# Layer 1's first product also of seven block products, summed in PSUM, with float32 weights kept in DRAM and GpSimd out of the weights

## The chip, the cores and the metric

The kernel runs on one core of a Trainium2 chip. The metric is the device time of one execution in microseconds (us), the median of three runs. The engines are named by their short names where rows are quoted: PE is TensorE's matmul, PEld its weight load, DVE VectorE, ACT ScalarE, POOL GpSimd, SP the engine that issues nearly all DMAs.

## The reference

Attention for 2 batches of 8 heads with 768 tokens of 64 values, masked by a hash bucket, and behind it two feed-forward layers on 1536 tokens of 512 values with 2048 hidden ones. The weights of both layers are float64.

```python
x = attn_out.transpose(0, 2, 1, 3).reshape(1536, 512)
h = x @ w_in;  sp = log1p(exp(min(h, 20)));  x = (h * tanh(sp)) @ w_out     # layer 1
h = x @ w_in2; return (h - tanh(h)) @ w_out2                                # layer 2
```

## The kernel before

Every float32 operand is kept as a high part, rounded to the matmul's float32r format, and a low part (the rest); a product is three matmuls: high by high, high by low, low by high. ScalarE makes high parts (a CAST), VectorE or GpSimd low parts (a subtraction).

**The order** is made by a planner (`Plan`). Each operation is handed in with an engine, an assumed cost, a key (a due time) and the buffers it reads and writes; the planner runs a list schedule over them, and the program is emitted in the order that comes out. Engines then work strictly in that order. The constants (UNIT, STEP, JIT, ...) set keys and costs only. SP's DMAs stand in one queue in that order too.

**Weights** arrive as 512 KB of float64 for 128 hidden units (`raw`). A conversion to float32 is four steps: VectorE masks the high word (TENSOR_SCALAR), VectorE merges sign and exponent (SCALAR_TENSOR_TENSOR), ScalarE scales the low word (ACTIVATE), and a sum joins them (on VectorE it shows as CUSTOM_DVE_ANT_0 or ISA, 128x1024 uint16). For layer 1 (`convert`) a split into high and low part follows at once, and all 32 tiles stay in SBUF (pools wa, wb, wc). For layer 2 (`fetch`) the sum is on GpSimd (L940), the float32 result is stored in DRAM, and each unit loads it back.

**Layer 1** (`feed_forward`, `hidden`, `outer`) goes over three blocks of 512 tokens and, in each, over 16 slices m of 128 hidden units: 12 matmuls of 512 columns make h (L823 to L825), ScalarE applies Mish and rounds (L838, L839), VectorE takes the low part (L842), and 12 matmuls of 512 columns add to four accumulators (L859).

**Layer 2** (`second_layer`, `unit`) goes over two halves of 768 tokens and 8 units of 256 hidden units each. A unit's first product is a 2x2 block product, made of seven block products (`product`) instead of eight: of each 6 matmuls with 384 columns (L1092 to L1094). That needs sums of the token blocks (t1 to t4, 22 GpSimd operations a half, in `tokens`) and of the weight blocks (s1 to s4, four GpSimd operations of 256 columns a unit). Five sums of products are made by VectorE from PSUM and SBUF (`plus`). Behind Tanh, 36 matmuls of 512 columns follow (L1143).

**PSUM**: tag s is one double bank, first for scores, then two accumulators; tag pt has six banks. In layer 1 two of the six are accumulators, in layer 2 four, which leaves two for the first product.

Of the kernel before, what the change touches and what calls it, by code (L numbers as in the profile page):

```python
# [39 lines left out]
N_A = 5  # L40
N_B = 3
N_PRE = 2
POOL_C = ((1, 4), (3,))
POOL_LAST = ((4,), (4,))
# [4 lines left out]

G_BUFS, E_BUFS, GX_BUFS, F_BUFS = 3, 3, 2, 2  # L50
T_BUFS, P_BUFS, U_BUFS = 3, 6, 3
# [3 lines left out]
EPS = 0.005  # L55
SPARE = 1
LATE = 0.22
LATS = 0.15
LATC = 1.0
# [6 lines left out]
MTICK = 5.53  # L66
# [13 lines left out]
OUT_LAG = 13.0  # L80
RAW = 12.0
C0 = 6.0
WB0 = 6

UNIT = 15.7
STEP = 1.06
OUT2 = 20.0
JIT = 18.0
DGL = 0.75
DY = 0.6  # L90
LATO = 1.0
FETCH = 30.0
CONV0 = -10.0
CONV2 = 5.2
TOK0 = 75.0
TOK1 = 70.0
UNIT0 = 0.0
TREL = 0.0
# [25 lines left out]
class Plan:  # L124
# [46 lines left out]
    def order(self):  # L171
        free, ready, done, queue = {}, {}, [], {}
# [23 lines left out]
        while len(done) < len(self.ops):  # L196
# [15 lines left out]
            o.start, o.end = t, t + o.cost  # L212
# [32 lines left out]
def tile_lsh_attention_moe(  # L245
# [52 lines left out]
    def slots(m0, m1):  # L298
        return " ".join(f"w{n}{m}" for m in range(m0, m1) for n in "io")

    for name, m0, m1 in (("wb", N_A, N_A + N_B), ("wc", N_A + N_B, KF)):
        for tag in slots(m0, m1).split():
            room(name, tag, 1)

    wd = (("a2", "a20 a21 a22 a23", 1), ("t2", "t2h t2l t3h t3l t4h t4l", 1), ("g2", "gh gl", 4), ("f2", "f2", 3))
    for name, tags, n in wd:
        for tag in tags.split():
            room(name, tag, n)

    room("raw", "raw", 2)  # L310
# [7 lines left out]
            ("const", "", 1), ("xy", "", 1), ("wa", slots(0, N_A), 1), ("t", "t", T_BUFS),   # L318
            ("g", "ph", G_BUFS), ("e", "pl", E_BUFS), ("f", "f", F_BUFS),
# [27 lines left out]
    def dma(nbytes, key, out, in_, reads=(), writes=(), release=0.0):  # L347

        op("DMA", max(0.55, nbytes / 180e3), key, lambda: nc.sync.dma_start(out=out(), in_=in_()), reads, writes, release=release)  # L349
# [317 lines left out]
    def finish(g, half, u, key):  # L667

        b, hp = pairs[g]
        r = rs[g, half]  # L670
        op(
            "POOL", 1.07, key + 0.2,
            lambda: nc.gpsimd.tensor_tensor(out=u(), in0=u(), in1=r(), op=ALU.mult),
            [r], [(u, 0), (u, 1)],
        )
        t0 = b * NT + half * TB
        cols = slice(t0 * P, (t0 + TB) * P)
        op("POOL", 0.5, key + 0.3, lambda: pool_copy(xh[hp][:, cols], u()), [(u, 0), (u, 1)], x_tok("xh", hp, t0, TB))
# [206 lines left out]

# [388 lines left out]
```

## Time and profile before

| | |
|---|---|
| time, median of 3 runs | 765.64 us (765.47 to 766.31) |
| the profiled execution | 765.25 us, its span 763.4 us |
| TensorE, VectorE, ScalarE, GpSimd busy | 746.7, 576.3, 462.5, 321.4 us |
| attention, layer 1, layer 2 | to about 235, 501 and 763 us |

The time is the device's for the whole execution; the span runs from the first to the last instruction. Busy time is the time in which an engine has at least one instruction under way; consecutive instructions of TensorE and VectorE overlap, so what one costs in a row of them is the distance of their starts, which is less than its duration.

### The profile page before, as it was taken

How to read it: one execution, taken by the hardware profiler on the slowest of the kernel's cores; microseconds unless marked ns; L12 is line 12 of the kernel's file. 1: busy time of each engine (PE TensorE's matmuls, PEld its weight loads, DVE VectorE, ACT ScalarE, POOL GpSimd, SP SyncE). 2: the span in 40 equal slices, each digit the busy share in tenths (PEclk: the TensorE clock that was granted, in tenths of full speed). 3: DMA queues.
4: the chain of work that ended last, by engine and by line, in shares of the span. 5: the costliest groups of instructions: out<-in, count | busy, mean ns of one | idle time of the engine just before them, and what ended most of it. 6: DMA issues, size and time to landing. Idle time of an engine off the chain costs nothing.

```text
span 763.4 us, 11533 instructions
## 1 busy us (share of the span) xinstructions
PE 746.7 (98%) x3853; PEld 650.9 (85%) x3853; DVE 576.3 (75%) x1044; ACT 462.5 (61%) x926; POOL 321.4 (42%) x346
## 2 busy tenths in 40 slices
PE   7999999999999899999999999999999999999998
PEld 5999999998988688888888888888887898889986
DVE  6999899899899898854443576669788877767743
ACT  6999899899897556653242435366455545445432
POOL 4787677677665200012222377434456321213000
PEclk9999999999999999999999999999999999999999
DMA  6674675665667630026565435632211124211002
GB/s 174 163 177 129 143 168 135 145 154 126 153 260 242 255 131 1 27 73 190 142 193 152 143 89 176 224 124 72 81 56 56 56 83 157 65 55 57 28 1 82
DMA packets 35559, 94.24 MB, mean 123 GB/s; under 512 B 5798, under 2 KB 8742, under 8 KB 35500
## 3 DMA queue, kind: packets, MB, share of 16 engines
q1 hardware_dynamic: 34924, 92.89, 41.6%
q8 instruction: 30, 0.49, 0.3%
q10 hardware_dynamic: 576, 0.62, 0.2%
q14 instruction: 29, 0.24, 0.1%
HBM read 63.01 MB, written 11.58 MB: 98 GB/s over the span
## 4 chain that ended last, share of the span: by engine, by line
PE 80%; DVE 8%; ACT 5%; DMA 3%; SPq 2%; issue 2%; ACTq 0%; DVEq 0%
PE pt L1143 11%; PE s L859 8%; PE pt L859 8%; PE pt L823 5%; PE pt L825 5%; PE pt L824 5%; PE pt L600 5%; PE s L1143 5%; PE pt L1092 4%; PE pt L1094 4%; PE pt L1093 4%; PE s L539 3%; PE s L540 3%; PE pt L578 3%; PE pt L579 3%; SPq L349 2%
## 5 line engine op out<-in xcount | busy, mean ns | idle before, releaser
L940 POOL TENSOR_TENSOR t<-t,raw 128x512 uint32<-128x512 uint32 x32 | 45.3, 1415 | 164.0 <-ACT raw L935 118.8
L543 DVE TENSOR_SCALAR_CACHE_REDUCE p<-s 128x768 f32<-128x768 f32 x93 | 88.3, 950 | 15.0 <-PE s L540 14.6
L565 ACT ACTIVATE p<-p,mn 128x768 f32<-128x768 f32 x96 | 90.5, 943 | 3.8 <-DVE p L543 2.1
L600 PE MATMUL pt<-cst,p 128*128 128x128 f32 x576 | 87.2, 274 | 2.3 <-ACT p L565 1.4
L898 POOL TENSOR_TENSOR f<-wi 128x256 f32<-128x256 f32 x32 | 30.4, 955 | 121.4 <-DVE a L898 33.2
L619 DVE TENSOR_TENSOR pl<-pt,ph 128x384 fp32r<-128x384 f32 x146 | 78.0, 548 | 4.7 <-ACT ph L616 3.7
L600 PEld LDWEIGHTS pt<-cst,p 128*128 128x128 f32 x576 | 70.6, 140 | 11.4 <-ACT f L608 3.3
L823 PE MATMUL pt<-xh,wi 128*128 128x512 f32 x192 | 75.6, 394 | 0.0
L825 PE MATMUL pt<-xh,wi 128*128 128x512 f32 x192 | 75.4, 393 | 0.0
L824 PE MATMUL pt<-xl,wi 128*128 128x512 f32 x192 | 75.3, 392 | 0.0
L616 ACT CAST ph<-pt 128x384 fp32r<-128x384 f32 x146 | 68.0, 480 | 9.2 <-PE pt L600 4.6
L578 PE MATMUL pt<-ph,vt 128*128 128x384 f32 x192 | 71.3, 371 | 0.4 <-DVE pl L619 0.4
L539 PE MATMUL s<-b,a 128*128 128x384 f32 x186 | 67.8, 364 | 1.7 <-DVE p L543 1.4
L838 ACT ACTIVATE f<-pt 128x512 f32<-128x512 f32 x34 | 20.3, 598 | 77.8 <-PE pt L825 77.6
L842 DVE TENSOR_TENSOR pl<-f,ph 128x512 fp32r<-128x512 f32 x34 | 28.4, 835 | 50.6 <-ACT ph L839 50.3
L579 PE MATMUL pt<-pl,vt 128*128 128x384 f32 x192 | 65.5, 341 | 0.0
L540 PE MATMUL s<-d,c 77*128 77x384 f32 (+1 forms) x186 | 63.2, 340 | 0.1
L859 PE MATMUL s<-ph,wo 128*128 128x512 f32 x192 | 59.7, 391 | 2.8 <-DVE wo L807 2.8
L859 PE MATMUL pt<-ph,wo 128*128 128x512 f32 x192 | 59.1, 389 | 0.0
L1107 ACT CAST gh<-pl 128x384 fp32r<-128x384 f32 x64 | 32.8, 514 | 29.6 <-DVE pl L898 28.9
L612 POOL TENSOR_TENSOR pl<-f,ph 128x384 fp32r<-128x384 f32 x46 | 48.5, 1054 | 2.5
L1105 ACT ACTIVATE f<-pl 128x384 f32<-128x384 f32 x48 | 25.2, 526 | 38.0 <-DVE pl L898 34.5
(256 smaller groups left out, 2060.5 us busy)
## 6 DMA issues: line engine op xcount, KB each, us to landing
wi<-in_moe_w_in_dram SPq DMA_DIRECT2D x16, 512.0 KB
wo<-in_moe_w_out_dram SPq DMA_DIRECT2D x16, 512.0 KB
raw<-in_moe_w_in_dram SPq DMA_DIRECT2D x16, 512.0 KB
w<-t SPq DMA_DIRECT2D x32, 256.0 KB
raw<-in_moe_w_out_dram SPq DMA_DIRECT2D x16, 512.0 KB
wi<-w SPq DMA_DIRECT2D x16, 512.0 KB
wo<-w SPq DMA_DIRECT2D x16, 512.0 KB
b<-kh SPq DMA_DIRECT2D x30, 192.0 KB
```

The lines of the kernel that those rows point to most:

```text
L539: nc.tensor.matmul(o, a()[:, tok], b_()[:, kc], start=True, stop=False)
L540: nc.tensor.matmul(o, c_()[used, tok], d_()[used, kc], start=False, stop=True)
L543: nc.vector.tensor_scalar(out=out, in0=in_, scalar1=MASKED, scalar2=None, op0=ALU.min, op1=ALU.min, accum_out=low)
L565: lambda: nc.scalar.activation(out=p(), in_=p(), func=AF.Exp, bias=mn(), scale=-1.0, accum_out=sm()[:, h, t:t + 1],),
L578: nc.tensor.matmul(o()[:, :HB], vt()[:, c, :], ph()[:, :HB], start=(c == 0), stop=False)
L579: nc.tensor.matmul(o()[:, :HB], vt()[:, c, :], pl()[:, :HB], start=False, stop=(c == NT - 1))
L600: nc.tensor.transpose(pt()[:, t * P:(t + 1) * P], pc[:, c * P:(c + 1) * P], ident)
L823: nc.tensor.matmul(h(), w()[:, 0, c], xh[kk][:, cols], start=(kk == 0), stop=False)
L824: nc.tensor.matmul(h(), w()[:, 0, c], xl[kk][:, cols], start=False, stop=False)
L825: nc.tensor.matmul(h(), w()[:, 1, c], xh[kk][:, cols], start=False, stop=(kk == KD - 1))
L859: nc.tensor.matmul(o, x, y, start=st and i == 0, stop=sp and i == 2)
L1143: nc.tensor.matmul(o, x()[:, i, c], w()[:, y], start=m == 0 and k == 0, stop=m == KF - 1 and k == 2)
```

## The change

Layer 1 takes the form that layer 2 has: two halves of 768 tokens, 8 units each, units numbered 0 to 31 over both layers. In its first half the first four units (PLAIN) make the 2x2 block product of eight block products; all others of seven. Layer 1's second product (`outer1`) works on 768 columns at once, as a matmul of 512 and one of 256 with the same weights. It has four accumulators in the 512s and two shared banks for the 256s, so two pt banks are left here too.

The seven products are summed in PSUM where that is possible: a copy by ScalarE starts a bank, and later products accumulate in it; two `plus` sums of five remain on VectorE. Layer 1's weights are converted to float32 for the first half, stored in DRAM, and loaded again for the second; each half splits them anew. All sums of conversions and of weight blocks are on VectorE, but those of units 0 and 1 (N_PRE), whose eight conversions lie in attention and end on GpSimd. The last pair's `finish` is on VectorE and ScalarE. Costs and keys in the planner are new; it also counts VectorE and GpSimd as slowing each other.

```diff
-POOL_LAST = ((4,), (4,))
+POOL_LAST = ((4,), ())
+SUMS = ("DVE", 0.34)
@@ order: VectorE and GpSimd slow each other in the plan
+            if o.eng == "DVE" and inside(o):
+                took += SLOW * min(took, max(0.0, free.get("POOL", 0.0) - t))
@@ finish
+        eng, cost, e = ("DVE", 0.55, nc.vector) if last else ("POOL", 1.07, nc.gpsimd)
@@ to_float, the conversion's last step (before: GpSimd in layer 2)
+        eng, cost, e = ("POOL", 1.45, nc.gpsimd) if pooled else ("DVE", 0.62, nc.vector)
+        op(eng, cost, key + 0.6, lambda: e.tensor_tensor(out=t(), in0=t(), in1=word(0), op=ALU.add), [raw], [tok], lat=LATF)
@@ unit_weights: layer 1's first half converts and stores, all others load
+            if (layer, sb) == (1, 0):
+                for side in range(2):
+                    i = 2 * part + side
+                    when = at(CONV_A + (4 * n + i) * CONV_S) if n < N_PRE else unit_at(n) - CONV1 + i * CSTEP
+                    to_float(
...
+                dma(P * DM * 8, when + CSTEP, lambda d=d: d.rearrange("p (m f) -> p m f", m=2), w32[part], both, there, rate=FAST)
@@ unit: plain, and seven products
+        if plain:
+            for k, (i, j) in enumerate(((1, 2), (2, 2), (1, 1), (2, 1))):
+                product(f"a{i}1", f"b1{j}", bank[k], True, key + 2 * st * k)
+                product(f"a{i}2", f"b2{j}", bank[k], False, key + 2 * st * k + st)
+                act(bank[k], i - 1, j - 1, key + 2 * st * k + st + 1)
+            return gs, outs
+        first, main, side = bank[:3]
...
+        product("a11", "b11", first, True, key)
+        keep(main, first, key + 1)
+        product("a12", "b21", first, False, key + st)
+        act(first, 0, 0, key + st + 1)
+        product("s2", "t2", main, False, key + 2 * st)
+        keep(u2, main, key + 2 * st + 1)
+        product("s1", "t1", side, True, key + 3 * st)
+        product("s3", "t3", main, False, key + 4 * st)
+        keep(w2, main, key + 4 * st + 1)
+        plus(h22, side, w2, key + 4 * st + 1.2)
+        act(h22, 1, 1, key + 4 * st + 1.3)
+        product("a22", "t4", main, False, key + 5 * st)
+        act(main, 1, 0, key + 5 * st + 1)
+        product("s4", "b22", side, False, key + 6 * st)
+        plus(h12, side, u2, key + 6 * st + 1)
+        act(h12, 0, 1, key + 6 * st + 1.2)
@@ outer1
+            for k, (y, x) in enumerate(((0, 0), (1, 0), (0, 1))):
+                st, sp = m == 0 and k == 0, m == KF - 1 and k == 2
+                nc.tensor.matmul(a()[:, n, :], w()[:, y, c], flat[x][:, :SEG], start=st, stop=sp)
+                nc.tensor.matmul(r()[:, 0, rest], w()[:, y, c], flat[x][:, SEG:], start=st and d % 2 == 0, stop=sp, skip_group_check=True)
```

How the change moves instructions is read from the program's order, engine by engine. TensorE before, where layer 1 has begun (wi and wo are weight tiles of slices m, ph and pl the high and low part behind Mish):

```order
L825 MATMUL pt<-xh_128,wi_4037 128x512
L859 MATMUL s<-ph,wo_3888 128x512 x2
L859 MATMUL s<-pl,wo_3888 128x512
L859 MATMUL pt<-ph,wo_3888 128x512 x2
L859 MATMUL pt<-pl,wo_3888 128x512
```

TensorE now, at unit 0's first second-product matmuls (a is a weight tile of the first product, o one of the second, gh and gl high and low part):

```order
L969 MATMUL pt<-xh_132,a_4266 128x384
L970 MATMUL pt<-xl_136,a_4266 128x384
L971 MATMUL pt<-xh_132,a_4266 128x384
L1033 MATMUL s<-gh,o_3783 128x512
L1034 MATMUL pt<-gh,o_3783 128x256
L1033 MATMUL s<-gh,o_3783 128x512
L1034 MATMUL pt<-gh,o_3783 128x256
L1033 MATMUL s<-gl,o_3783 128x512
L1034 MATMUL pt<-gl,o_3783 128x256
```

So each step of 512 columns in the second product has one of 256 behind it, and the first product goes in steps of 384. VectorE before, at the end of attention, ahead of the weight tile that the second slice's second product needs (wo_4177):

```order
L775 TENSOR_SCALAR t<-wi_3852 128x512
L783 SCALAR_TENSOR_TENSOR t<-wi_3852,t 128x512
L800 ISA t<-wo_3763,t 128x1024
...
L800 ISA t<-wi_3852,t 128x1024
...
L807 TENSOR_TENSOR wo_4161<-t,wo_4161 128x512
L775 TENSOR_SCALAR t<-wo_3938 128x512
L807 TENSOR_TENSOR wo_4177<-t,wo_4177 128x512
```

VectorE now, from just behind attention's last gathers to unit 0's low halves (w is a float32 weight tile, t2l to t4l and xl the low parts of token blocks):

```order
L695 TENSOR_TENSOR xl_138<-u,xh_134 128x384
L769 TENSOR_TENSOR a_4266<-w_2184,a_4266 128x512
L800 SCALAR_TENSOR_TENSOR w_4207<-raw,w_4207 128x512
L769 TENSOR_TENSOR gl<-pl,gh 128x384
L769 TENSOR_TENSOR a_4272<-w_2184,a_4272 128x512
L769 TENSOR_TENSOR o_4289<-w_2606,o_4289 128x512
L769 TENSOR_TENSOR gl<-pl,gh 128x384
L769 TENSOR_TENSOR o_4300<-w_2606,o_4300 128x512
L769 TENSOR_TENSOR t4l<-t,t4h 128x384
L769 TENSOR_TENSOR gl<-pl,gh 128x384 x2
```

There the conversions of slices 2 to 5 stood; now splits for unit 1 and parts of unit 2's conversion stand between unit 0's low halves. GpSimd now, behind its last work for attention's seventh pair: the block sums of layer 1's first half begin here, with two operations of the last pair among them.

```order
L695 TENSOR_TENSOR xl_137<-u,xh_133 128x384
L769 TENSOR_TENSOR t<-xh_131,xl_135 128x384 x2
L355 TENSOR_SCALAR ph<-f 128x384
L769 TENSOR_TENSOR t<-t 128x384
L624 TENSOR_TENSOR pl<-f,ph 128x384
L769 TENSOR_TENSOR t<-xh_133,xl_137 128x384
```

Before, the last pair's `finish` stood there, behind it twenty sums of layer 2's conversions (L940), and only then layer 2's block sums.

## Rows read from the trace of the kernel before

**Rows 1.** The page's head: span, busy time of the engines.
```profile
span 763.4 us, 11533 instructions
PE 746.7 (98%) x3853; PEld 650.9 (85%) x3853; DVE 576.3 (75%) x1044; ACT 462.5 (61%) x926; POOL 321.4 (42%) x346
```
**Rows 2.** Busy time by stage: stretch, its length, engines, granted clock, DMA share, GB/s.
```profile
235.00:501.00 266.00, 262.57 (x1153) 215.79 (x1153) 172.31 (x255) 123.64 (x219) 83.27 (x67) 0.99 0.44 145
501.00:764.00 263.00, 255.53 (x1261) 227.44 (x1259) 193.05 (x316) 128.56 (x253) 75.76 (x73) 1.00 0.21 68
```
**Rows 3.** Shorter stretches, columns PE, PEld, DVE, ACT, POOL, clock, DMA.
```profile
251.00:267.00 16.00, 13.21 (x51) 10.09 (x50) 13.26 (x22) 8.07 (x15) 2.58 (x3) 0.89 0.76 298
...
560.00:590.00 30.00, 28.14 (x140) 24.80 (x139) 27.04 (x39) 15.06 (x32) 16.80 (x15) 1.00 0.21 71
155.00:182.00 27.00, 26.72 (x177) 24.92 (x176) 24.50 (x56) 24.75 (x57) 18.70 (x25) 1.00 0.61 145
209.00:236.00 27.00, 26.44 (x162) 23.00 (x160) 25.33 (x56) 24.56 (x52) 17.22 (x17) 1.00 0.70 246
283.00:299.00 16.00, 16.00 (x72) 13.25 (x71) 13.87 (x26) 9.09 (x17) 0.00 (x0) 1.00 0.00 1
```
**Rows 4.** TensorE's waits, 205 to 272 and 498 to 764 us: total, times, longest.
```profile
PE s L859 <- DVE wo L807: 2.8, 1, 2.8
...
PE pt L1092 <- DVE pl L898: 3.0, 3, 1.1
```
**Rows 5.** TensorE in order of time, 250 to 264 us: start, duration, instruction.
```profile
256.11 0.63 PE L823 MATMUL pt<-xh,wi 128*128 128x512 f32 x1
256.54 0.63 PE L824 MATMUL pt<-xl,wi 128*128 128x512 f32 x1
...
261.64 0.39 PE L823 MATMUL pt<-xh,wi 128*128 128x512 f32 x1
...
263.91 0.39 PE L824 MATMUL pt<-xl,wi 128*128 128x512 f32 x1
```
**Rows 6.** TensorE in order of time, 581 to 583 us, layer 2.
```profile
581.09 0.34 PE L1092 MATMUL pt<-wi,a 128*128 128x384 f32 x1
...
582.66 0.63 PE L1143 MATMUL s<-wi,gh 128*128 128x512 f32 x2
```
**Rows 7.** The chain that ended last, 204 to 206 us: transposes.
```profile
204.70 0.98 PE pt L600 x9
```
**Rows 8.** VectorE by form, 272 to 327 us, GpSimd idle: count, busy, mean ns.
```profile
L783 DVE SCALAR_TENSOR_TENSOR t<-wo,t 128x512 uint32<-128x512 uint32 x10 | 6.9, 688 | 0.1
...
L800 DVE CUSTOM_DVE_ANT_0 t<-wi,t 128x1024 uint16<-128x1024 uint16 x10 | 6.8, 685 | 0.0
...
L775 DVE TENSOR_SCALAR t<-wo 128x512 uint32<-128x512 uint32 x10 | 4.2, 423 | 0.1
```
**Rows 9.** VectorE in order of time, 505 to 525 us.
```profile
509.98 0.68 DVE L898 TENSOR_TENSOR wi<-wi,wi 128x512 fp32r<-128x512 f32 x1
510.58 0.69 DVE L898 TENSOR_TENSOR a<-wi,a 128x512 fp32r<-128x512 f32 x1
...
523.05 0.55 DVE L898 TENSOR_TENSOR gl<-pl,gh 128x384 fp32r<-128x384 f32 x1
523.52 0.55 DVE L898 TENSOR_TENSOR pl<-pt,ph 128x384 f32<-128x384 f32 x1
```
**Rows 10.** VectorE by form, 560 to 590 us, GpSimd busy.
```profile
L898 DVE TENSOR_TENSOR gl<-pl,gh 128x384 fp32r<-128x384 f32 x7 | 5.8, 833 | 0.1
...
L898 DVE TENSOR_TENSOR raw<-wo,raw 128x512 fp32r<-128x512 f32 x2 | 2.5, 1226 | 0.0
...
L898 DVE TENSOR_TENSOR a<-wi,a 128x256 fp32r<-128x256 f32 x1 | 0.4, 411 | 0.0
```
**Rows 11.** GpSimd's groups of block sums and conversion sums, whole span.
```profile
L940 POOL TENSOR_TENSOR t<-t,raw 128x512 uint32<-128x512 uint32 x32 | 45.3, 1415 | 164.0 <-ACT raw L935 118.8 <-DVE t L927 45.3
...
L898 POOL TENSOR_TENSOR t<-t 128x384 f32<-128x384 f32 x8 | 10.6, 1330 | 0.2
```

More of the change, by code (lines that the diff above doesn't have):

```diff
@@ L171, in order, with inside @@
     def order(self):
-        free, ready, done, queue = {}, {}, [], {}
+        free, ready, done, queue, running = {}, {}, [], {}, {}
+        def inside(o):
+            return o.cost > 0.3 and not any(b.pool.startswith("ps_") for b in o.bufs)
         for o in sorted(self.ops, key=lambda o: (o.key, o.n)):
@@ L786, in convert @@
             ),
[L787 removed]
+            [raw], [tok], lat=LATF,
         )
         op(
[L790 to L797 removed]
@@ L1066, in unit_weights @@
         outs = []
         for i in range(2):
[L1068 to L1070 removed]
+            tl = buf("oo" if odd else "oe", f"o{i}", [P, 2, DM], F32R)
+            eng, cost, e = ("DVE", 0.62, nc.vector)
@@ L1075, in tile_lsh_attention_moe, with unit @@
     W = slice(0, HB)
-    def unit(sb, u, ops):
-        n = sb * NU + u
+    def unit(layer, sb, u, ops):
+        n = number(layer, sb, u)
         key = unit_at(n)
-        A, outs = unit_weights(sb, u)
+        plain = "t1" not in ops
+        A, outs = unit_weights(layer, sb, u, plain)
         gs = [[buf("g2", x, [P, 2, HB], F32R) for x in ("gh", "gl")] for _ in range(2)]
@@ new lines, in half @@
+    def half(layer, sb, keys, slack):
+        outer, n_out, dt = (outer1, KD, 1.05) if layer == 1 else (outer2, NT, 0.69)
+        acc = None
+        for u in range(NU):
+            n = number(layer, sb, u)
+            if not u:
+                ops = blocks(sb)
+            if u == (PLAIN if n < NU else 0):
+                ops = tokens(layer, sb, keys, slack)
+            gs, outs = unit(layer, sb, u, ops)
+            if acc is None:
+                wide = buf("ps_s", "s", [P, 2, XB])
+                acc = [(wide, 0), (wide, 1)] + [(buf("ps_t", "pt", [P, 1, XB]), 0) for _ in range(NT - 2)]
+            key = unit_at(n) + OUT2
+            for i in range(2):
+                for t in range(n_out):
+                    k = key + dt * (n_out * i + t if u < NU - 1 else 2 * t + i)
+                    outer(2 * u + i, gs[i], outs[i], acc, k, t)
+        (keep if layer == 1 else leave)(sb, acc, unit_at(n) + OUT2 + 1.0)
@@ new lines, in tile_lsh_attention_moe @@
+    for layer in (1, 2):
+        for sb in range(B):
+            if layer == 1 and sb == 0:
+                keys, slack = (lambda i: unit_at(0) + TOK_A + i * TOK_S), 0.0
+            else:
+                keys, slack = (lambda i, n=number(layer, sb, 0): unit_at(n) - TOK_L + i * TOK_T), 0.0
+            half(layer, sb, keys, slack)
+        if layer == 1:
+            for u in range(NU):
+                for i, (part, side) in enumerate(itertools.product(range(2), range(2))):
+                    fetch(2, 2 * u + side, part, unit_at(NU) - CONV0 + (4 * u + i) * CONV2)
```

551 lines of the change are left out of this document (204 added, 347 removed).

## The prediction

> **What bounds the kernel now.** I read the page's head first: TensorE is busy in 98% of the span, VectorE in 75% [rows 1]. The reader is to see in it that little can be won by waiting less: TensorE's own work must shrink, or nothing large happens. Then the stretches: layer 1 (235 to 501 us) and layer 2 (501 to 764) hold 262.6 and 255.5 us of TensorE work [rows 2], and in a quiet piece of layer 1 TensorE is busy all of 16.00 us while VectorE is busy 13.87 [rows 3]. So in layer 1 only the number of matmul columns, and what VectorE can no longer keep up with, count.
>
> Then TensorE's waits. Between attention and layer 1 one wait of 2.8 us for VectorE's half of a weight [rows 4], and behind it matmuls at 0.43 us where they later take 0.227 [rows 5], with a mean granted clock of 0.89 in that stretch [rows 3]: 1.2 GHz for some 8 matmuls, 1.6 us. The passage costs 4.4 us. In layer 2, 3.0 us in three waits for VectorE [rows 4], two of them where GpSimd is busy 16.8 of 30 us and TensorE only 28.14 [rows 3].
>
> **What a matmul costs.** From start to start: 512 columns, ten from 261.64 to 263.91 us, 0.227 us [rows 5]. 384 columns, nine from 581.09 to 582.66, 0.1744 [rows 6]. 128 columns, nine in 0.98 us, 0.109 [rows 7]. The changed kernel also has matmuls of 256 columns, which the trace doesn't show: not under 0.109 (half the columns) and not over 0.174 (half as many more). I take the line through 384 and 512, 0.122 us, since the same kind of operands stands on it.
>
> The 128-column row lies above that line (0.07), so something else than columns bounds it; at 256 columns the line is above 0.109 and would still rule. The Trainium skill, "TensorE: Matmul & The Clock Gate", section "LDWEIGHTS (loading the stationary operand)", gives columns divided by 1.2, an estimate of 107 ns for 128; the trace agrees with it in the 109 ns. By the page's gap formula a 256-column matmul would take 109 ns, and the sum below would be 5.0 us lower; I stay with the line.
>
> **The change, part by part.**
>
> *Layer 1's matmuls.* Removed: 576 first-product and 576 second-product matmuls of 512 columns, 1152 x 0.227 = 261.5 us. Added: four plain units of 48 and twelve of 42 matmuls with 384 columns, 696 x 0.1744 = 121.4; second product 384 x 0.227 = 87.2 and 384 x 0.122 = 46.8. Sum 255.4: **6.1 us less**. The bounds of the 256-column price make it 11.1 less or 13.9 more.
>
> *Layer 2's matmuls* stay 672 and 576: nothing.
>
> *Attention.* Eight weight conversions now lie in it from the third pair on; before, six started in the last pair. On VectorE each has two steps, 0.42 and 0.69 us alone [rows 8]. Less the 0.08 by which neighbours overlap (512 wide: 0.69 long, 0.60 apart [rows 9]) that is 0.95 us, 7.6 in all over some four pairs. VectorE is busy 24.50 of 27 us there and reaches 25.33 in the last pair [rows 3], so it has 0.8 us to spare in a pair, 3.3 in four. Lower bound: nothing, if they fall into its gaps; upper: 7.6. A row for the full case is the last pair, where TensorE is busy 26.44 instead of 26.72 [rows 3]: 0.3 us for a full pair, though with layer-1 matmuls filling in. I take **2 us more**. The third step is on GpSimd (18.70 busy of 27), which hides it.
>
> *The passage.* Before, VectorE stood in a row of some thirty conversion steps when the first second-product matmul needed its weight; now units 0's and 1's float32 weights are ready, and what is queued ahead is the splitting of units 0 and 1 and the conversions of units 2 to 4. From the gather of attention's last half but one (the u<-pt ahead of the rows shown of VectorE's order) to unit 1's last low half, 40 rows on, I count 5 masks at 0.34, 5 merges and 5 sums at 0.60, 7 splits at 0.60 and 22 of 384 columns at 0.47 [rows 8, 9]: 22 us. TensorE has from the same point to unit 1's second product about 29 us of matmuls. Against that lead stand GpSimd's 22 block sums, 1.33 us each [rows 11], two thirds of them behind that gather. In 560 to 590 us VectorE's instructions with both inputs in SBUF were held up so: 0.833 instead of 0.55, 1.226 instead of 0.69 [rows 9, 10]; over all of them some 7 us for 16.8 of GpSimd, 0.42 for 1. Here that is 20 x 0.42 = 8. So 30 against 29: a wait of 0 to 7 us, I take 2 in place of 4.4, **2.4 us less**.
>
> The Trainium skill, "SBUF — State Buffer", section "Who interferes with whom", says that such an instruction and a GpSimd one that reads SBUF block each other wholly, for the first one's duration. The rows agree that only instructions with two SBUF inputs suffer (one with PSUM among its inputs keeps 0.55 [rows 9]) but the mean loss is under half. By the rule the 20 us of GpSimd would all be lost: a rival below.
>
> *Layer 1's units.* Per seven-product unit VectorE has 12 conversion steps (6.2 us), four 256-wide sums at 0.33 (0.41 [rows 10] less the overlap), splits of 3.4, four low halves 1.9, two block sums 0.9: 13.7 of the unit's 42 x 0.1744 + 24 x 0.349 = 15.7 us. Over the first half my count of its order is 106 us up to unit 7's last low half, and 12 + 8 more for two sets of block sums: 126 against 129 of TensorE. That is tight. Bounds: nothing, and 8 us if it loses as much as 560 to 590 (1.86 in 30 us) over all 129. In layer 1 ScalarE alone frees an accumulator bank, so lateness reaches TensorE a unit later, in the second product; I take **2 us more**.
>
> *Layer 2.* Weight sums leave GpSimd, the conversions' last step too (45.3 us of it [rows 11]); three of five PSUM sums move from VectorE to ScalarE copies, busy 128.6 of 263 us there [rows 2]. The four GpSimd weight sums of a unit go to VectorE for 1.3 us, the three that leave give back 1.4. The three waits with some 0.3 us that each adds until matmuls run at their pace again are 4 us; I take half: **2 us less**, bounds 0 and 4.
>
> *Stores and reloads* of layer 1's weights, 16 more pairs of 512 KB on SP, replace nothing that TensorE waits for: DMA was busy 21% in 560 to 590 [rows 3]. SP's stores wait for conversions, with reads behind them; four raw buffers cover that. Without the cover a unit waits a landing, which the first half's 8 us contain.
>
> Sum: -6.1 +2 -2.4 +2 -2 = -6.5. On the profiled execution's 765.25 us that is 758.75; the runs' median is 765.64, 0.4 above, so **759 us**.
>
> **Rivals.**
> *Everything hides* (0.15): attention and layer 1 cost nothing, the passage waits nothing: -6.1 -4.4 -4 = -14.5, 751. For it: in 283 to 299 us VectorE at 13.87 of 16 costs TensorE nothing. Against: two free banks now, four then.
> *VectorE bounds layer 1's first half* (0.20): 8 us there and 4 in attention: -6.1 +4 -2.4 +8 -2 = +1.5, 767. For it: the 126 of 129; against: the order puts conversions ahead of their need. It ends slower than before from 8 us above the forecast on (the gain of 6.5 and the 1.5 of the measurement).
> *GpSimd's block sums hold VectorE wholly* (0.05): 20 us lost at the passage instead of 8, and 5 more later: 759 + 17 = 776. Against: the 7 us lost in 16.8 [rows 3, 10]. The Trainium skill's page "SBUF — State Buffer" states it as the rule.
> *256-column matmuls cost what 384 do* (0.06): weights would have to bind them. -6.5 + 384 x 0.052 = +13.5: 779, slower; the gain is gone from 0.139 us. For it: nothing but that 128 columns lie above the line.
>
> **How the numbers follow.** Forecast 0.54, by itself 754 to 763. A measurement of this kernel tells 0.2%, 1.5 us. Faster: the forecast but for 0.02 at its end, the first rival and 0.09 of the second, 0.76. Same: that 0.02 and 0.06 of the second, 0.08. Slower: 0.05 of the second and the last two, 0.16. Range 750 to 769: the last two rivals and the outer ends of the first two are left out.
>
> **What would show it.** Right: 512-column second products 0.227 and 256-column 0.122 apart; layer 1 some 258 to 262 us; no wait over 2 us near 250 us and no stretch at half the clock; block sums still slowing VectorE. Wrong: 256-column steps near 0.17; TensorE waiting for low halves unit after unit in layer 1; attention ending over 3 us later; or layer 2 losing where GpSimd left.

## The result

The changed kernel takes 769.8 us (median of 4 runs, 768.17 to 770.31), the kernel before 765.56 (764.95 to 766.31): ratio 1.0056, 95% interval 1.0043 to 1.0068. It is 0.56% slower; the forecast was 759 and the range ended at 769. The profiled execution took 768.17 us against 765.25.

The page's head of the changed kernel (answers to rows 1):

```profile
span 766.4 us, 12378 instructions
...
PE 741.7 (97%) x4165; PEld 675.3 (88%) x4165; DVE 638.9 (83%) x1260; ACT 525.0 (69%) x1104; POOL 269.3 (35%) x274
```

TensorE's busy time fell by 5.0 us and the span grew by 3.0: the work did shrink, and TensorE stands still 8 us longer. The stretches of the changed kernel, with the columns of rows 2 and 3 (stretch, length, PE, PEld, DVE, ACT, POOL, granted clock, DMA share, GB/s):

```profile
235.00:501.00 266.00, 256.37 (x1456) 238.53 (x1455) 243.69 (x441) 173.87 (x359) 77.32 (x48) 0.99 0.57 187
501.00:764.00 263.00, 258.74 (x1290) 231.26 (x1288) 179.05 (x339) 140.37 (x291) 22.23 (x16) 1.00 0.24 81
...
155.00:182.00 27.00, 26.42 (x176) 24.93 (x175) 25.46 (x57) 25.49 (x57) 23.13 (x28) 1.00 0.71 185
209.00:236.00 27.00, 25.82 (x168) 24.15 (x167) 26.11 (x58) 23.70 (x53) 10.83 (x12) 1.00 0.42 121
236.00:252.00 16.00, 12.36 (x73) 10.99 (x71) 15.29 (x26) 8.87 (x19) 12.06 (x11) 1.00 0.40 124
252.00:268.00 16.00, 13.79 (x67) 12.47 (x68) 11.82 (x23) 10.92 (x22) 7.64 (x4) 0.89 0.32 98
283.00:299.00 16.00, 16.00 (x95) 15.02 (x94) 16.00 (x33) 10.23 (x21) 1.54 (x1) 1.00 0.79 259
300.00:316.00 16.00, 12.74 (x65) 11.68 (x64) 11.80 (x23) 8.58 (x17) 11.86 (x6) 0.89 0.58 192
560.00:590.00 30.00, 30.00 (x151) 26.93 (x150) 23.40 (x45) 17.73 (x38) 3.58 (x4) 1.00 0.21 71
```

Two places stand out: the passage from attention to layer 1 (236 to 268 us), and a hole in layer 1 at 300 to 316 us, which the kernel before has nothing like (rows 2: TensorE 262.57 of 266 busy). In the hole VectorE, gapless just before (16.00 of 16), idles too, while GpSimd is busy 11.86 of 16 us. Both stretches have a granted clock of 0.89: part of each ran at 1.2 GHz behind a wait of about 3 us. TensorE's waits, whole span (total, times, longest):

```profile
PE pt L969 <- ACT pt L1002: 3.5, 2, 3.3
...
PE pt L969 <- ACT a L937: 2.8, 1, 2.8
PE pt L969 <- DVE ph L769: 2.3, 2, 2.1
PE pt L591 <- DVE pl L631: 2.1, 1, 2.1
```

**The hole, engine by engine.** TensorE, in order of time:

```profile
305.11 0.28 PE L1034 MATMUL pt<-gl,o 128*128 128x256 f32 x1
305.23 0.39 PE L1033 MATMUL pt<-gh,o 128*128 128x512 f32 x1
305.46 0.28 PE L1034 MATMUL pt<-gh,o 128*128 128x256 f32 x1
...
306.15 0.28 PE L1034 MATMUL pt<-gl,o 128*128 128x256 f32 x1
309.69 0.45 PE L969 MATMUL pt<-xh,a 128*128 128x384 f32 x1 [3.26 <-ACT pt L1002]
```

ScalarE, whose copy L1002 it waits for:

```profile
304.19 0.51 ACT L868 CAST t3h<-t 128x384 fp32r<-128x384 f32 x1 [4.24 <-POOL t L769]
...
305.71 1.21 ACT L808 ACTIVATE raw<-raw 128x512 uint32<-128x512 uint32 x2
...
309.17 0.47 ACT L1002 COPY pt<-pt 128x384 f32<-128x384 f32 x1
```

GpSimd, for whose block sum ScalarE stood 4.24 us:

```profile
297.45 5.61 POOL L769 TENSOR_TENSOR t<-xh,xl 128x384 f32<-128x384 f32 x1 [18.57 <-DVE xl L769]
303.15 2.11 POOL L769 TENSOR_TENSOR t<-t 128x384 f32<-128x384 f32 x2
```

And VectorE, first in the passage, then around the hole:

```profile
239.30 1.36 DVE L800 SCALAR_TENSOR_TENSOR w<-raw,w 128x512 uint32<-128x512 uint32 x1
...
242.68 1.44 DVE L812 CUSTOM_DVE_ANT_0 w<-raw,w 128x1024 uint16<-128x1024 uint16 x1
244.04 1.34 DVE L688 TENSOR_TENSOR u<-u,r 128x384 f32<-128x384 f32 x1
...
301.78 0.42 DVE L769 TENSOR_TENSOR f<-w 128x256 f32<-128x256 f32 x1
306.40 1.46 DVE L812 CUSTOM_DVE_ANT_0 w<-raw,w 128x1024 uint16<-128x1024 uint16 x1 [4.20 <-ACT raw L808]
```

Read upwards: TensorE waits for a copy on ScalarE; the copy stands behind the rounding of t3, a block sum of layer 1's second half, whose first reader on TensorE comes 75 us later (at 379.05); the rounding waits for a GpSimd sum that takes 5.61 us where most take 1.0 to 1.35. The sum started while VectorE ran gapless and ended 0.9 us after VectorE's last instruction had ended at 302.2. VectorE stopped only because its next instruction needs ScalarE's scaling L808, which stands behind the same rounding. The three wait in a ring that opens only when VectorE runs out of work. In the kernel before the longest block sum took 1.47 us. (The prediction and the text ahead of it speak of 22 block sums a half on GpSimd; the traces have 16 a half in both kernels.)

A late sum isn't enough for such a hole. A sum of 5.68 us in the passage held a rounding on ScalarE even longer:

```profile
267.06 0.51 ACT L868 CAST t3h<-t 128x384 fp32r<-128x384 f32 x1 [4.45 <-POOL t L769]
```

There TensorE waited for nothing: the matmuls that it had ahead needed nothing from behind that rounding. At 306 us it had come to the first unit with seven products, which needs ScalarE's copy L1002 between its first two.

To divide the loss I add up, over successive TensorE instructions, the distance of their starts less what the same width takes in a quiet row: 0.227 us for 512 columns in layer 1 of the kernel before, 0.230 in the later ones, 0.231 elsewhere, 0.116 for 256, 0.174 for 384, 0.109 for 128. The columns are what remains by stage in each profiled execution, in us; lines named e_ are the experiments below.

| version | median, us | 16–224 | 224–272 | 272–500 | 500–764 |
|---|---|---|---|---|---|
| before | 765.56 | 11.3 | 6.2 | 0.4 | 5.2 |
| after | 769.8 | 14.2 | 9.5 | 5.8 | 4.4 |
| e_lat6 | 767.35 | 15.2 | 7.2 | 6.7 | 3.5 |
| e_sums_vec | 762.37 | 15.1 | 6.3 | -0.4 | 7.1 |
| e_plain8 | 763.82 | 14.9 | 8.9 | -0.3 | 3.6 |
| e_finish_pool | 769.46 | 14.9 | 11.6 | 3.7 | 7.2 |
| e_pool_late | 771.95 | 15.9 | 6.6 | 11.9 | 4.0 |
| e_sv_late | 756.76 | 16.1 | 2.8 | 0.7 | 3.5 |
| e_noconv | 768.41 | 12.5 | 9.1 | 6.9 | 5.5 |
| e_place_pool | 769.46 | 14.7 | 13.5 | 4.1 | 3.4 |
| e_sv2 | 757.09 | 14.4 | 6.6 | -0.4 | 2.5 |
| e_sv2_late | 752.56 | 14.0 | 2.8 | -0.3 | 1.4 |
| e_sv2_late_p3 | 756.98 | 15.6 | 2.8 | 3.7 | 2.5 |

From before to after: attention 2.9 more, passage 3.3 more, layer 1 5.4 more, layer 2 0.8 less, in all 10.8; the matmuls give 7.2 (below); 3.6 us are left, and the profiled execution is 2.9 longer (0.7 us over 4165 steps is what rounding the quiet steps to some 0.2 ns leaves open). Attention's column moves by up to 2 us between versions whose instructions there stand in the same order (e_sv_late and e_sv2_late), so of it only larger differences count. Layer 2's column moves as well: 3.4 to 7.2 in the versions with its block sums on GpSimd.

### The profile page after: what moved, and what is told of

The parts are those of the page before. It is cut to its first block, busy times and chain, and to the rows that moved or that the text cites. A ratio compares the mean times of both kernels' runs of the same rounds, so it can differ in the third digit from the quotient of the medians.

```text
span 766.4 us, 12378 instructions
## 1 busy us (share of the span) xinstructions
PE 741.7 (97%) x4165; PEld 675.3 (88%) x4165; DVE 638.9 (83%) x1260; ACT 525.0 (69%) x1104; POOL 269.3 (35%) x274
## 4 chain that ended last, share of the span: by engine, by line
PE 75%; DVE 15%; ACT 3%; issue 3%; POOL 2%; DMA 2%; SPq 0%; ACTq 0%; DVEq 0%
PE pt L1046 11%; PE pt L969 8%; PE pt L971 8%; PE pt L970 8%; PE pt L612 7%; PE s L1046 5%; PE pt L1033 4%; PE pt L1034 4%; PE s L1033 4%; PE s L551 4%; PE s L552 3%; PE pt L590 3%; PE pt L591 3%; DVE p L555 2%; POOL t L769 2%
## 5 line engine op out<-in xcount | busy, mean ns | idle before, releaser
L769 POOL TENSOR_TENSOR t<-xh,xl 128x384 f32<-128x384 f32 x32 | 62.1, 1944 | 230.9 <-DMA w<-t 145.1
L969 PE MATMUL pt<-xh,a 128*128 128x384 f32 x288 | 97.9, 340 | 8.6 <-ACT pt L1002 3.5
L971 PE MATMUL pt<-xh,a 128*128 128x384 f32 x288 | 97.9, 340 | 0.1
L970 PE MATMUL pt<-xl,a 128*128 128x384 f32 x288 | 97.3, 338 | 0.0
L1046 PE MATMUL pt<-o,gh 128*128 128x512 f32 x256 | 79.6, 392 | 0.0
L769 DVE TENSOR_TENSOR gl<-pl,gh 128x384 fp32r<-128x384 f32 x128 | 74.7, 589 | 3.7 <-ACT gh L988 3.4
L1034 PE MATMUL pt<-gh,o 128*128 128x256 f32 x256 | 72.0, 281 | 0.0
L988 ACT CAST gh<-pl 128x384 fp32r<-128x384 f32 x128 | 64.8, 512 | 4.1 <-DVE pl L769 3.3
L969 PEld LDWEIGHTS pt<-xh,a 128*128 128x128 f32 x288 | 54.6, 190 | 14.4 <-ACT pt L1002 4.2
L769 DVE TENSOR_TENSOR pl<-pt,f 128x384 f32<-128x384 f32 x32 | 17.8, 557 | 50.4 <-ACT f L986 50.4
L970 PEld LDWEIGHTS pt<-xl,a 128*128 128x128 f32 x288 | 54.6, 190 | 1.8
L971 PEld LDWEIGHTS pt<-xh,a 128*128 128x128 f32 x288 | 54.5, 189 | 0.9 <-DVE a L769 0.9
```

Source lines behind the costliest of these rows:

```text
L769: eng.tensor_tensor(out=out, in0=in0, in1=in1, op=ALU.subtract if sub else ALU.add)
L969: nc.tensor.matmul(o, tl()[:, 0, c], at_(0, kk), start=start and kk == 0, stop=False, skip_group_check=not start)
L970: nc.tensor.matmul(o, tl()[:, 0, c], at_(1, kk), start=False, stop=False, skip_group_check=not start)
L971: nc.tensor.matmul(o, tl()[:, 1, c], at_(0, kk), start=False, stop=kk == 1, skip_group_check=not start)
L1034: nc.tensor.matmul(r()[:, 0, rest], w()[:, y, c], flat[x][:, SEG:], start=st and d % 2 == 0, stop=sp, skip_group_check=True)
L1046: nc.tensor.matmul(o, x()[:, i, c], w()[:, y], start=m == 0 and k == 0, stop=m == KF - 1 and k == 2)
```

## The experiments

Theory 1: a GpSimd block sum is held by a gapless VectorE, and the harm comes through the queues of ScalarE and VectorE, where other work stands behind the sum's result. Theory 2, the rival on record: VectorE's own work bounds layer 1's first half. Theory 3: contention in the passage is the loss.

**e_lat6**: the planner expects a GpSimd sum's result later (one more line, not shown, keeps GpSimd's own queue out of it).

```diff
+LATP = 6.0
-op("POOL", 1.0, key, lambda: add(nc.gpsimd, ...), [...], [x[i]])
+op("POOL", 1.0, key, lambda: add(nc.gpsimd, ...), [...], [x[i]], lat=LATP)
```

> The planner now assumes that what leaves a GpSimd block sum reaches the other engines after 6 us (before, 0.6). Only the order of the queues changes: ScalarE's roundings of the sums and VectorE's low halves behind them are placed later, the work is the same. Theory 1 (a GpSimd block sum takes 5 to 7 us beside a gapless VectorE, and ScalarE's queue stands behind its rounding, then VectorE, then TensorE): TensorE's 3.3 us wait at 306 us and the slow matmuls behind it go, some 4 us, so about 765.5; the block sums themselves still take 5 us and more in that stretch. Theory 2 (VectorE's own work bounds layer 1's first half): the same work in another order wins nothing, 769 to 771, and waits for VectorE come back elsewhere in 270 to 370 us. Theory 3 (the loss is in the passage from attention to layer 1, from contention): the wait at 251 us stays, no more than 1 us won.

Measured: 767.35 us, ratio to before 1.0025 (1.0013 to 1.0037). The passage gets 2.3 us cheaper, but the hole stays: 3.9 us at 305. GpSimd there:

```profile
283.20 18.00 POOL L770 TENSOR_TENSOR t<-xh,xl 128x384 f32<-128x384 f32 x1 [6.05 <-DVE t4l L770]
301.28 1.02 POOL L770 TENSOR_TENSOR t<-t 128x384 f32<-128x384 f32 x1
```

A sum of 1.0 us lasted 18.00. My "5 to 7 us" was no property of the sum: it lasts as long as VectorE leaves no gap, so no latency in a planner covers it.

**e_sums_vec**: layer 1's block sums on VectorE.

```diff
-op("POOL", 1.0, key, lambda: add(nc.gpsimd, tmp(i), ...
+on, on_e = (("DVE", 0.47), nc.vector) if layer == 1 else (("POOL", 1.0), nc.gpsimd)
+op(*on, key, lambda: add(on_e, tmp(i), ...
```

> Layer 1's 32 block sums stand on VectorE instead of GpSimd, at some 0.41 to 0.47 us each: 16 in each half, so 7 us more for VectorE in each half, and nothing of GpSimd beside the two-input SBUF instructions. Theory 1: the stretched sums are gone, so no wait for a block sum's rounding at 306 us; VectorE's instructions in the passage lose their stretch (1.34 and 1.44 us back to 0.6 and 0.7); 763 to 767. Theory 2 (VectorE bounds the first half, 126 us before against 129): 7 us more put it over TensorE's work, so layer 1's first half ends 4 us or more later, 773 to 777, with TensorE waiting for VectorE unit after unit in 270 to 370 us.

Measured: 762.37, ratio 0.9961 (0.9949 to 0.9973), 7.4 us below the changed kernel. Its stretches:

```profile
236.00:252.00 16.00, 13.13 (x77) 11.74 (x76) 15.62 (x35) 10.72 (x23) 1.87 (x2) 1.00 0.35 111
252.00:268.00 16.00, 15.41 (x81) 14.47 (x81) 14.85 (x30) 12.28 (x26) 0.00 (x0) 0.89 0.40 119
300.00:316.00 16.00, 16.00 (x94) 15.06 (x93) 15.97 (x34) 11.48 (x24) 0.00 (x0) 1.00 0.71 242
```

The hole is gone although VectorE has 16 sums more in each half; it is busy 15.97 of 16 us while TensorE waits for nothing. Theory 2 falls. (VectorE's whole busy time rose by 1.9 us only, from 638.9 to 640.8, because its instructions are no longer stretched.) Theory 3 holds for its part: the passage gains 3.2 us and is back at what the kernel before has there, 6.3 against 6.2.

**e_plain8**: `PLAIN = 4` becomes `8`.

> All eight units of layer 1's first half are plain, so its block sums, their roundings and low halves, and the weight sums of four units fall out of the first half; four units get 6 matmuls of 384 columns more each, 24 x 0.174 = 4.2 us of TensorE. Layer 1's second half and layer 2 are as in the changed kernel. Theories 1 and 3: the 5.9 us that layer 1's first half lost against its matmuls, and most of the 3 us that the passage got dearer, come back: 8 less, 4.2 more, about 766. Should only the event at 306 us come back: 769 to 770. Theory 2 would also gain here (a plain unit leaves VectorE idle), but then the gain lies all behind 270 us and the passage keeps its two waits of 2 to 3 us.

Measured: 763.82, ratio 0.9982 (0.997 to 0.9994). The first half loses nothing from 272 us on. The passage keeps 8.9: GpSimd now does eight of the second half's sums there, since its queue holds nothing else and the planner's later key doesn't delay it. The other eight run from 300 us on, one of them in 7.83 and one in 5.94 us:

```profile
300.00:316.00 16.00, 16.00 (x95) 15.02 (x94) 14.43 (x22) 8.96 (x18) 13.83 (x6) 1.00 0.66 208
```

```profile
317.85 5.94 POOL L769 TENSOR_TENSOR t<-xh,xl 128x384 f32<-128x384 f32 x1 [3.78 <-DVE t4l L769]
```

ScalarE waits for none of them and TensorE loses nothing: here held sums have no urgent work behind their results.

**e_finish_pool**: `last = g == len(pairs) - 1` becomes `False`.

> The finish of attention's last pair stands on GpSimd again as in the kernel before; all else is as changed. If its move to VectorE is what made the passage dearer (4.4 us before, about 9 after), 2 to 4 us come back and the time is 766 to 768. If the passage waits because block sums and VectorE's two-input SBUF instructions hold each other up, GpSimd has more to do at the same place and it gets worse: 770 to 773.

Measured: 769.46, ratio 1.0057 (1.0042 to 1.0072). The passage is dearer by 2.1 us, the hole smaller by as much. So the finish's move was not the loss.

**e_micro** and **e_micro2**: VectorE rows with one GpSimd sum, behind the program's end. The second differs in the buffers that VectorE writes (the sum's own are set apart too, not shown):

```diff
-nc.vector.tensor_tensor(out=o, in0=xh[0][:, 0:XB], in1=xh[1][:, 0:XB], op=ALU.add)
+nc.vector.tensor_tensor(out=row_out(), in0=xh[0][:, 0:XB], in1=xh[1][:, 0:XB], op=ALU.add)
```

> The changed kernel, and behind its last output some rows that measure the contention by itself (nothing of the computation is left out; the time of the whole says nothing). A GpSimd sum of 384 columns (as the block sums) is released by VectorE's fifth instruction of a gapless row: three sums alone first; then beside a row of 20 sums of 512 columns with both inputs in SBUF, beside 20 masks with one SBUF input, beside 20 sums with PSUM and SBUF, beside rows of five SBUF sums and one with PSUM; last, eight GpSimd sums in a row with eight VectorE sums of two SBUF inputs in their midst. Theory 1 (a gapless row of VectorE instructions with two SBUF inputs keeps GpSimd out until it ends): the GpSimd sum takes about 1.0 us alone and beside the PSUM row, and 11 to 13 us beside the SBUF row; in the mixed row it ends within some 4 us, at the first instruction with PSUM; VectorE's instructions keep 0.6 us while GpSimd is held. The rule I had used in the prediction (GpSimd's sums slow VectorE's instructions by some 0.42 us for each us of theirs, and themselves run on): 1.0 to 1.5 us in every row, VectorE's sums 0.8 to 1.3 us beside it.

> The same rows as in the first measurement, but VectorE's instructions write four buffers in turn. In the first one they all wrote one buffer and followed each other at 0.73 us, longer than their own 0.69: each waited for the end of the one before, so the rows had holes, and GpSimd's sum took 1.30 us. In layer 1 they follow each other at 0.60. Theory 1: with the holes closed GpSimd's sum beside 20 sums of two SBUF inputs takes 10 us or more and VectorE keeps 0.60; beside the PSUM row 1.0; in the mixed row it ends at the first instruction with PSUM among its inputs. Rival (the two engines take turns, whatever the row): 1.3 us again and VectorE's spacing about 1.3 while it lasts; then the 5 to 18 us in the kernel have another cause than the row.

Measured: with holes (first) GpSimd took 1.00 to 1.30 us in every row. Without holes: 1.30 beside 20 sums, 7.41 beside 20 masks, 1.00 beside the PSUM row, 3.72 in the mixed row, and 5.52 for the first of eight beside eight SBUF sums. Neither the theory's 10 us nor the rival's 1.3 throughout; that VectorE's inputs lie in SBUF doesn't decide it alone. The mixed row came out as theory 1 had it: the sum ended at 829.28, 0.94 us behind the start of the first instruction with PSUM (828.34).

**e_pool_late** and **e_sv_late**: `TOK_A = 0.0` becomes `20.0`, in the changed kernel and in e_sums_vec.

> The changed kernel with the first half's block sums (still on GpSimd) and their splits keyed 20 us later, out of the passage and into layer 1's units. Theory 1: the passage gets 2 us or more cheaper, but the sums now all meet a gapless VectorE: several of them take 5 to 20 us, and TensorE loses 4 us or more behind 270 us; in all 768 to 775. If the sums were only slowed to some 1.3 us and the passage were the only place where they do harm: 764 to 766, with no wait over 1 us behind 270 us.

> The kernel with layer 1's block sums on VectorE (762.4), and in the first half these and their splits 20 us later. In the passage of that kernel VectorE has ahead of the low halves that TensorE waits for two low halves of block sums, one block sum and two conversion steps. If what stands in VectorE's queue there makes the passage's 6 us, 1 to 3 us of it go: 759.5 to 761.5. If the passage is set by the finish and the split of attention's last rows, nothing goes: 762 to 763. If VectorE after all has no room in layer 1's first half, waits come up in 270 to 330 us: over 764.

Measured: on GpSimd 771.95, ratio 1.0084 (1.0068 to 1.01); on VectorE 756.76, ratio 0.9886 (0.9871 to 0.99). The same edit costs 2 us on one engine and gives 5.6 on the other. On GpSimd eight sums still ran at 239 to 249 us (the queue holds nothing else), the others met the gapless VectorE, and layer 1 lost 11.9 us. On VectorE the key does set the place, and the passage falls from 6.3 to 2.8: non-urgent sums and their splits had stood ahead of the low halves that TensorE needs.

**e_noconv**: the mask and merge of the attention's eight conversions left out (the merge's line is changed likewise, and the sum then reads the scaled word twice; not shown).

```diff
-op("DVE", 0.4, key, lambda: nc.vector.tensor_scalar(...
+pooled or op("DVE", 0.4, key, lambda: nc.vector.tensor_scalar(...
```

> The changed kernel with the two VectorE steps of the eight weight conversions inside attention left out (units 0 and 1 of layer 1's first half then multiply by wrong weights; what is left, the scaling on ScalarE and a sum on GpSimd, takes its usual place). It prices the attention term by itself. As I forecast (2 us for eight conversions): attention's last scores end about 2 us sooner and the time is 767 to 768.5. If their whole 7.6 us lie on the path: 762 to 763. If they hide: 769.5 to 770.5. The waits at 251 and 306 us should stay in each case by theory 1.

Measured: 768.41, ratio 1.0043 (1.0026 to 1.006). Attention loses 12.5 instead of 14.2 us, 1.7 for the eight, and the median falls by 1.4. Attention's column moves by as much of itself, so this bounds the term (it is not 7.6) rather than sizes it. The hole stays, with a wait of 4.7 us.

**e_place_pool**: the roundings and low halves of the first half's sums on GpSimd too.

```diff
+if layer == 1 and sb == 0:
+    op("POOL", 1.0, key, lambda: pool_copy(at_(0, k), tmp(i)), [x[i], *gate], hi)
+    op("POOL", 1.0, key + 0.1, lambda: add(nc.gpsimd, at_(1, k), tmp(i), at_(0, k), True), [x[i], *hi], lo)
+    return
```

> The changed kernel; the roundings (ScalarE) and low halves (VectorE) of the first half's block sums stand on GpSimd too, so that no other engine has an instruction in its queue that waits for a late block sum until unit 4 needs the tiles. The sums stay where they are and GpSimd gets 16 instructions more. Theory 1 (the harm comes through ScalarE's and VectorE's queues): sums may still take 5 us and more, but the wait of 3.3 us at 306 us and the slow matmuls behind it go, about 764 to 766, unless the chain becomes so late that unit 4 waits. If the sums harm TensorE through contention with VectorE alone: GpSimd's added work makes it worse, 770 to 775.

Measured: 769.46, ratio 1.0052 (1.0039 to 1.0065). Its stretches:

```profile
252.00:268.00 16.00, 10.51 (x40) 9.92 (x41) 15.97 (x15) 10.53 (x21) 15.60 (x14) 0.68 0.10 33
300.00:316.00 16.00, 15.57 (x89) 14.03 (x87) 16.00 (x24) 9.51 (x20) 8.71 (x7) 1.00 0.49 148
```

The hole is gone, and layer 1 loses 4.1 us instead of 5.8. But this run can't part the theories as its expectation says. The edit moves the roundings of the first half's sums alone (`sb == 0`). The rounding in the hole is one of the second half's, and it still stands on ScalarE, behind GpSimd's sum:

```profile
303.99 0.51 ACT L872 CAST t3h<-t 128x384 fp32r<-128x384 f32 x1 [0.16 <-POOL t L769]
```

```profile
301.20 1.33 POOL L769 TENSOR_TENSOR t<-xh,xl 128x384 f32<-128x384 f32 x1
```

What changed is that GpSimd, with its added work, came to that sum at 301.20 instead of 297.45 and was served in 1.33 us instead of 5.61. So the run shows once more where the wait comes from, not the way it takes. Sums of 4.5 and 4.75 us still occur later. In the passage GpSimd is now busy 15.60 of 16 us, VectorE gets through 15 instructions instead of 23, and TensorE waits 3.8 and 2.0 us; the granted clock there is 0.68, and what was won is lost.

**e_sv2_late** and **e_sv2_late_p3**: all block sums on VectorE, those of layer 1's first half 20 us later; then `PLAIN = 3` too.

> All block sums on VectorE, layer 2's 32 too, and those of the first half 20 us later. Against the kernel that did so for layer 1 alone (756.8): if GpSimd's sums are what delays VectorE at the head of layer 2 (TensorE waits 0.6 and 1.1 us there, 2.2 in the changed kernel), 1 to 2 us go: 755 to 756. If VectorE's own work at that place is the bound, 3.5 to 4 us more work for it in each half make it 757 to 759.

> The same with three plain units in layer 1's first half instead of four: 6 matmuls of 384 columns less, 1.05 us of TensorE. VectorE was busy 111 of 112 us in 272 to 384 us with four plain units. If that is still room: 1 us below the kernel before it, 754 to 755. If VectorE is now the bound (the rival that I gave 0.20, but with the sums on VectorE): waits for VectorE between 290 and 370 us, and no gain or a loss of 1 to 4 us.

Measured: 752.56, ratio 0.9831 (0.9818 to 0.9844); and 756.98, ratio 0.9889 (0.9876 to 0.9902). e_sv2_late beats both kernels, by 13.0 and 17.2 us. Its stretches, then its VectorE where the changed kernel's is shown above:

```profile
235.00:501.00 266.00, 264.38 (x1527) 247.47 (x1526) 250.73 (x510) 184.11 (x377) 2.01 (x2) 1.00 0.60 198
...
236.00:252.00 16.00, 14.66 (x87) 13.34 (x85) 14.29 (x29) 10.48 (x20) 1.27 (x2) 1.00 0.61 184
252.00:268.00 16.00, 15.72 (x90) 14.86 (x91) 15.23 (x31) 13.46 (x30) 0.00 (x0) 1.00 0.42 145
...
300.00:316.00 16.00, 16.00 (x94) 14.89 (x93) 15.87 (x34) 11.08 (x23) 0.00 (x0) 1.00 0.64 205
```

```profile
237.74 0.69 DVE L800 SCALAR_TENSOR_TENSOR w<-raw,w 128x512 uint32<-128x512 uint32 x1
...
239.71 0.68 DVE L812 CUSTOM_DVE_ANT_0 w<-raw,w 128x1024 uint16<-128x1024 uint16 x1
...
242.09 0.55 DVE L688 TENSOR_TENSOR u<-u,r 128x384 f32<-128x384 f32 x1
```

The same merge, conversion and normalisation take half of the time: 0.69, 0.68 and 0.55 us instead of 1.36, 1.44 and 1.34. The granted clock is 1.00 in all stretches. I expected 1 to 2 us against e_sv_late and measured 4.2; by the table 1.0 is in layer 1, 2.1 in layer 2, and 2.1 in attention, where nothing differs in the order, so that part isn't explained. With three plain units layer 1 loses 3.7 us with VectorE at 110.7 of 112 us: the edge that theory 2 feared is there, one plain unit further on. (TensorE waits there for ScalarE's copies, so that VectorE is the cause is argued only.)

**e_micro3**: twenty rows of four kinds, and five moments for the GpSimd sum.

> Behind the last output of the changed kernel, twenty gapless VectorE rows, each with one GpSimd sum of 384 columns released just ahead of it: five rows each of 12 sums with two SBUF inputs, 20 masks (one SBUF input), 12 merges (two SBUF inputs), and 3 times sum, mask, merge, sum, as in layer 1. The five differ in the width (64 to 448 columns) of one PSUM instruction ahead, that is in when GpSimd's sum comes to the row. Nothing of the computation is left out. If the row alone decides: the five of a kind agree, masks holding GpSimd for the row's 6.8 us, sums and merges letting it in at once (1.3 us). If the moment decides (who is at the port first): among the rows of sums and merges both 1.3 us and 5 to 7 us occur, with VectorE losing some 0.7 us where GpSimd comes in and nothing where it is held.

GpSimd's sums, and under them VectorE's rows beside them:

```profile
778.00 8.16 POOL L1173 TENSOR_TENSOR d<-d,xh 128x384 f32<-128x384 f32 x1 [9.45 <-DVE d L1169]
789.16 0.99 POOL L1173 TENSOR_TENSOR d<-d,xh 128x384 f32<-128x384 f32 x1 [3.01 <-DVE d L1169]
...
822.30 7.54 POOL L1173 TENSOR_TENSOR d<-d,xh 128x384 f32<-128x384 f32 x1 [10.05 <-DVE m L1170]
832.85 1.27 POOL L1173 TENSOR_TENSOR d<-d,xh 128x384 f32<-128x384 f32 x1 [3.01 <-DVE d L1169]
```

```profile
778.00 7.30 DVE L1147 TENSOR_TENSOR m<-xh,xh 128x512 f32<-128x512 f32 x12
...
789.26 8.06 DVE L1147 TENSOR_TENSOR m<-xh,xh 128x512 f32<-128x512 f32 x12
...
822.20 6.79 DVE L1150 TENSOR_SCALAR m<-xh 128x512 uint32<-128x512 uint32 x20
...
832.85 7.59 DVE L1150 TENSOR_SCALAR m<-xh 128x512 uint32<-128x512 uint32 x20
```

The moment counts. In the twelve rows that the sum reached 0.1 us or more ahead it took 0.99 us and VectorE lost 0.56 to 0.76 (8.06 instead of 7.30). In the eight where it came within some 0.1 us of the row's first instruction it got in after one instruction (1.27 to 1.54) four times, and four times, once in each kind, it was held until the row had ended (7.26 to 8.16) while VectorE lost nothing. Masks, which read SBUF once, hold it as sums do. Within these 0.1 us it stays open which of the two happens: among the sums the one that came with the row's first instruction was held (778.00), among the masks one 0.1 us behind it (822.30 against 822.20). In e_micro2 the sum came some 0.22 us behind the row's start and was held in three of four rows with SBUF inputs. The Trainium skill, "SBUF — State Buffer", section "Who interferes with whom", says that who issues first has the shared port for the whole instruction and the other blocks, and that such a mask can be in a mode that takes this port. The rows agree on both, and go further: a gapless row can keep it from instruction to instruction.

**e_sv2**: as e_sv2_late, with `TOK_A = 0.0`.

> All block sums on VectorE at the places of the changed kernel (not 20 us later). It parts the engine from the place. If the passage's loss in the kernel with layer 1's sums on VectorE (762.4) came from the place, as the comparison with 756.8 says, it stays here, and layer 2's head gives its 2 to 4 us: 757.5 to 760.5. If 752.6 came from layer 2's sums alone: 753 to 755.

Measured: 757.09, ratio 0.9899 (0.9881 to 0.9916); the passage keeps 6.6 us. So of the 17.2 us between the changed kernel and the best, the engine makes 12.7 on this way (layer 1's sums 7.4, layer 2's 5.3) and the place in VectorE's queue 4.5. On the way over e_sv_late the steps are 7.4, then 5.6 for the place and 4.2 for layer 2's sums, and attention's own movement is in all of these.

## Why the prediction was wrong

Against the terms of the sum, the passage came out 5.7 us worse, layer 1's units 3.4, layer 2 1.2 and attention 0.9, the matmuls 1.1 better: 10.1 in all, from 6.5 less to 3.6 more. In the two largest it is the way of GpSimd's block sums to TensorE that I had wrong: in the passage by a lead that was to cover them, in layer 1's units by taking them to be off the path.

*Layer 1's matmuls* (6.1 us less): right in kind. A 512 and a 256 step follow each other in 0.346 us (three pairs from 305.11 to 306.15), so 384 x 0.346 + 696 x 0.1744 = 254.3 against 261.5: 7.2 less. The 256-column step is 0.116, between my 0.122 and the 0.109 of the other estimate.

*Layer 1's units* (2 us more): 5.4. That lies within the bounds of 0 to 8, but by luck, since the mechanism is another. I asked only whether VectorE has the time (126 of 129 us), and it has: in e_sums_vec it has 16 sums more in each half, and TensorE loses nothing from 272 to 500 us. I took GpSimd's sums as fixed at 1.33 us, off the path, with VectorE the only one to lose. Rows 10 showed one direction of the contention; the kernel before has gaps in VectorE's row where GpSimd works (rows 3: 27.04 of 30 us), its longest block sum took 1.47 us, and so it never showed the other. The very number that I read as "tight" was the warning: with VectorE at 16.00 of 16 us a sum can be held for 5.61 us, and ScalarE's queue stands behind it. The rival for contention (776) had the loss on VectorE's side. That GpSimd's sum is the source is shown by e_sums_vec. That the wait runs through the rounding in ScalarE's queue is read from the rows of the hole, and e_plain8 fits it (sums of 7.83 and 5.94 us that ScalarE doesn't wait for, and no loss); no run moved that rounding alone.

*The passage* (2.4 us less): 3.3 more, the largest miss. The rate of the contention was right: in 239 to 253 us six VectorE instructions were stretched by 4.3 us in all for 9.4 us of GpSimd, 0.46 for 1, against my 0.42. Its amount was less than the 8 us for 20 that I had set. What failed is the lead. I set 30 us of VectorE against 29 of TensorE up to unit 1's second product, but TensorE stops before: 2.1 us for attention's own last low half, and 2.8 us for unit 1's first weights, behind which the clock falls again. Instructions that TensorE needs in order can't draw on the lead to a later one. And I took the splits and sums ahead of these as given; e_sv_late shows that their place costs 3.5 us.

*Attention* (2 us more): 2.9, and 1.7 of it goes with the conversions in e_noconv. In the eleven versions that keep them the column is 2.7 to 4.8 above that of the kernel before, so 2 was probably low.

*Layer 2* (2 us less): 0.8, which its column's own movement doesn't tell from 2. The three waits of 3.0 us in rows 4 became one of 2.1 (at 541 us). Ahead of the sum of products that TensorE waited for there, four VectorE instructions took 1.37 to 1.50 us beside GpSimd's block sums, where they take 0.55 to 0.69 alone. With these sums on VectorE the column is 1.4 to 2.5, with them on GpSimd 3.4 to 7.2. So I had the wrong ones of GpSimd's instructions in mind: the block sums that stayed, not the weight sums that left.

Of the signs of right, the matmul steps and the block sums' slowing of VectorE came true; "no wait over 2 us near 250 us and no stretch at half the clock" did not, and layer 1 didn't shrink: from attention's last matmul to layer 1's last one it was 264.8 us (244.85 to 509.60) and is 270.0 (248.23 to 518.19), each with some of layer 2's first matmuls in it. "Everything hides" (751), to which I gave 0.15, is near in number to e_sv2_late, but that kernel has its sums elsewhere, and attention there is still 2.7 us dearer. The change was worth it, but not with the block sums on GpSimd.

## What to carry to other kernels

A helper engine off the path is only as good as the gaps of the one it shares memory with: when work is added to VectorE until it has no gaps, move GpSimd's work beside it to VectorE too, or expect it to come late by as long as the row lasts (18 us here). Look for what stands behind a late result in in-order queues: here a rounding whose result TensorE didn't need for 75 us stopped three engines, while a sum held for 7.83 us with nothing urgent behind it cost nothing. And when an order is made by keys, check that the queue has something else in it; on an empty queue a later key delays nothing.

## What the runs showed of the hardware

A GpSimd sum of 0.99 us lasted 18.00 beside VectorE instructions that followed each other without a gap, and in equal rows either 0.99 to 1.54 or 7.26 to 8.16. It took 0.99 whenever it came 0.1 us or more ahead of the row; with the row's start or up to 0.23 us behind it, it was let in or held. VectorE sums that all write one buffer follow each other at 0.73 us instead of 0.60, and in the rows with such holes GpSimd's single sum never took more than 1.30.
